# Attention and a long convolution on one core: the middle of every sixth VectorE exponential block computed on GpSimd

## The chip, the cores and the metric

The kernel runs on one core of a Trainium2 chip. The metric is the device time of one execution in microseconds (us). A core has a matrix engine (TensorE, PE in the profile), VectorE (DVE), ScalarE (ACT), GpSimd (POOL) and SyncE (SP), which only starts transfers here. Each engine works through its own list of instructions in order, and they wait for one another by semaphores. TensorE writes into PSUM, eight banks of 128 x 512 fp32; everything else lies in SBUF.

## The reference

Two independent halves are computed in bf16 and put side by side (S = 2048 rows, D = 512 columns each):

```python
# A: attention, 32 heads of 16 columns
qkv = x @ wqkv                      # q, k, v: [32, 2048, 16]
p = softmax(q @ k^T / 4)            # [32, 2048, 2048]
a = (p @ v) @ wo

# B: a gated convolution
kv = shift_conv(k, shift_k, 4 taps) * v
y = causal_conv(kv, ssm_k, 2048 taps per channel) + kv * ssm_D
b = q * y
out = concat([a, b], axis=-1)       # [2048, 1024]
```

## The kernel before

**Attention.** The score matrix is cut into 2048 blocks of 128 keys x 512 queries. A block takes a score matmul into a PSUM bank (L729), an exponential into SBUF, and a matmul with V (L795) that adds it to an accumulator bank. The softmax's denominators come out of the same matmul, from columns of ones beside V; a finished group of 64 blocks is transposed, divided and put away on VectorE (L820 to L835).

**The convolution** is 8192 small matmuls (L920) against rows of the kernel that SyncE loads, 512 loads of 512 KB (L903). They fill TensorE's time between score matmuls at a planned pace of one step (four matmuls) in `PACE` ns. VectorE moves results (L936, L962).

**Who does the exponential.** A step (`T`) has two or three blocks in neighbouring banks. ScalarE takes two or three of them in one instruction (L736). At some steps the third goes to VectorE instead, which computes 2^z in five passes (`exp_on_dve`): from PSUM to an integer that holds exponent and fraction (tile `EI`, L754), a linear pass over the low 16 bits into fp32 (tile `EM`, L757), twice a sum times itself in place (L759), and a last pass that adds the exponent and stores bf16 bits (tile `PTD`, L760):

```python
js = [job(... u = PA * f + PB ...)]            # L757
for c in (PC, PD): js.append(job(... u = (u + c) * u ...))   # L759
js.append(job(... PTD = ei * 2.0 ** -9 + u ...))             # L760
```

The first pass frees the PSUM bank, which the score matmuls two steps later need. `EI` and `PTD` have four buffers each, `EM` two.

**What sets the order.** All instructions of a core are laid out before the run by a planner in the same file. It keeps a clock for each engine with fixed costs (692 ns for a VectorE pass from PSUM, 427 for the linear one) and writes out each engine's list. VectorE's work consists of jobs with a due time; whenever the planned VectorE is free, `commit_one` takes the ready job that is due first. A block's last pass is due 7000 ns after its step's exponential. A step's third block is given to VectorE if the cost of all pending passes is below `DVE_OPEN` and enough blocks are left (`form`, L1138). The run follows the written order whatever the true times are.

**GpSimd** sets up masks and fills in the first 5 us. Later it only starts transfers: shifted rows of k, the q columns, `wo`, and the stores of output rows. In time it idles for most of the run.

Of the kernel before, what the change touches and what calls it, by code (L numbers as in the profile page):

```python
# [6 lines left out]
ALU = mybir.AluOpType  # L7
BF16 = mybir.dt.bfloat16
FP32 = mybir.dt.float32
INT32 = mybir.dt.int32  # L10
UINT16 = mybir.dt.uint16
# [30 lines left out]
PA, PB, PC, PD = -1.32672387e-05, -6.76483421, 6.76469236, -6.64090344  # L42
# [12 lines left out]
DVE_GAP = 2  # L55
DVE_OPEN = 3000.0
DVE_END = 48
PACE = 357.0
LAG_NS = 130.0
PE_SLACK = 850.0  # L60
PV_NS = 260.0
DMA_NS = 5600.0
N_TAIL = 9
# [75 lines left out]
def at_of(h):  # L139
    return 0.0 if h is None else Eng.at.get((id(h[0]), h[1]), 0.0)  # L140
# [13 lines left out]
def bass_concat_heads__mha_block__ssm_conv_h3__prompt_kernel(  # L154
# [21 lines left out]
    def sem(name):  # L176
        return enter(nc.semaphore(name))

    def sb(name, shape, dt=BF16):
        return enter(nc.sbuf_tensor(name, shape, dt))  # L180
# [12 lines left out]
    WKV = sb("WKV", [128, 2, 4, D])  # L193
# [8 lines left out]
    PTD = sb("PTD", [128, 4, QB])  # L202
    EI = sb("EI", [128, 4, QB], INT32)
    EM = sb("EM", [128, 2, QB], FP32)
    JNK = sb("JNK", [128, 2], FP32)
    WK = WKV[:, 0, :, :]
    WV = WKV[:, 1, :, :]
    WOP = WKV[:, 0, :, :]
    wr_flat = WR[:, :, :].rearrange("p r w -> p (r w)")
    KZS = wr_flat[:, 0:4 * LKZ].rearrange("p (c m) -> p c m", c=4)  # L210
# [12 lines left out]
    pe, act, dve, pool, sp = [Eng(sem(n), *k) for n, k in (("s_pe", (170.0,)), ("s_act", (100.0,)), ("s_dve", (-10.0, -85.0)),  # L223
                                                           ("s_pool", ()), ("s_sp", ()))]

    jobs = []
    WAIT = Job(None, (), 0.0, 0.0)

    def job(fn, deps, cost, due, then=None):
        j = Job(fn, deps, cost, due, then)  # L230
        jobs.append(j)
        return j

    def resolve(j):
        out = []
        for d in j.deps:
            d = d() if callable(d) else d
            if isinstance(d, Job):
                if d.h is None:
                    return None  # L240
                d = d.h
            out.append(d)
        return out

    def ready_of(j):
        deps = resolve(j)
        return None if deps is None else max([0.0] + [at_of(d) + 45.0 for d in deps if d is not None])

    def commit_one(until=None):
        found = [(ready_of(j), j) for j in jobs]  # L250
        found = [(r, j) for r, j in found if r is not None]
        if not found:
            return False
        t0 = max(dve.t, min(r for r, j in found))
        if until is not None and t0 >= until:
            return False
        j = min((j for r, j in found if r <= t0), key=lambda j: j.due)
        for r, u in sorted(((r, u) for r, u in found if u.due < j.due), key=lambda x: x[1].due):
            if r < t0 + j.cost and t0 + j.cost + u.cost + 80.0 > u.due:
                j = u  # L260
                break
        jobs.remove(j)
        j.h = dve.op(j.fn, resolve(j), cost=j.cost)
        if j.then:
            j.then(j.h)
        return True

    def advance(t):
        while commit_one(t):
            pass  # L270
# [36 lines left out]
    def dma(eng, dsem, outp, inp, deps=(), transpose=False):  # L307
        h = dsem.add()

        def fn(e):  # L310
            f = e.dma_start_transpose if transpose else e.dma_start
            f(outp, inp).then_inc(dsem.sem, 16)  # L312
        eng.op(fn, deps, inc=False)
        return h
# [18 lines left out]
    def load_x(eng, ds, t0, t1):  # L333
        return dma(eng, ds, KV[:, t0:t1, :], x2[t0 * 128:t1 * 128, :].rearrange("(t p) d -> p t d", p=128))

    def landing(h, us):
        Eng.at[(id(h[0]), h[1])] = 1000.0 * us
        return h
# [3 lines left out]
    h_wk = [landing(dma(act, d_w[1], WK[:, :, 0:128], wview[:, :, D:D + 128]), 5.4)]  # L342
    h_wv = landing(dma(act, d_w[2], WV, wview[:, :, 2 * D:3 * D]), 8.5)
    h_xn[1] = landing(load_x(sp, d_x[1], 4, 8), 8.5)
# [97 lines left out]
    def pe_unit(u, bank, dcs=(0, 1, 2, 3)):  # L442
        kind = u[0]
        deps = [bank_free[bank]]
        if kind == "q":
# [3 lines left out]
            def mm(e, dc):  # L449
                return e.matmul(PS[:, bank, :], lhsT=WQ[:, dc, o * 128:(o + 1) * 128], rhs=xT[:, dc, qb * 512:(qb + 1) * 512],  # L450
                                start=(dc == 0), stop=(dc == 3))
# [7 lines left out]
        else:  # L459
# [3 lines left out]
            def mm(e, dc):  # L463
                return e.matmul(PS[:, bank, :], lhsT=xT[:, dc, kt * 128:(kt + 1) * 128], rhs=WV[:, dc, :],  # L464
                                start=(dc == 0), stop=(dc == 3))
# [141 lines left out]
    def turn_first(cs, t0, dep):  # L607
        def fn(e):
            ins = None
            for c in cs:  # L610
                for t in range(t0, t0 + 2):
                    pbf = PS[:, first_bank[c], :].bitcast(BF16)
                    ins = e.transpose(pbf[:, 128 * t:128 * t + 128],
                                      KV[:, t, 128 * c:128 * c + 128], IDN[:, :])
            return ins
        return pe_op(fn, [dep, h_idn], full(128, 2 * len(cs)))
# [3 lines left out]
    for c in range(4):  # L620
        h = turn_first([c], 2, h_xn[0])
# [9 lines left out]
    def first_q(dc):  # L631
        return pe_op(lambda e: e.matmul(PS[:, 6, :], lhsT=WQ[:, dc, 0:128], rhs=xT[:, dc, 0:512],
                                        start=(dc == 0), stop=(dc == 3)), [h_x[0][dc], h_wq[0]], full(512, 1))

    def first_k(bank, c0, c1):
        def fn(e):
            ins = None
            for dc in range(4):
                ins = e.matmul(PS[:, bank, c0:c1], lhsT=WK[:, dc, 0:128], rhs=xT[:, dc, c0:c1],
                               start=(dc == 0), stop=(dc == 3))  # L640
            return ins
        return pe_op(fn, [*h_x[0], h_wk[0], bank_free[bank]], full(c1 - c0, 4))

    for dc in range(4):
        h = first_q(dc)
    evac_unit(("q", 0, 0), 6, h)
    h = first_k(7, 0, 128)
# [68 lines left out]
    h_blk = {}  # L716
# [28 lines left out]
    h_fix = {}  # L745
    h_ptd = {}
    h_pair = {}

    def exp_on_dve(b, bank, h, T):
        i = on_dve[b]  # L750
        u, ei = EM[:, i % 2, :], EI[:, i % 4, :]
        f = ei.bitcast(UINT16).rearrange("p (n h) -> p n h", h=2)[:, :, 0]
        end = at_of(h_exp[T])
        h_fix[i] = job(lambda e: e.tensor_scalar(ei, PS[:, bank, :], FIX_LO, FIX_ADD, ALU.max, ALU.add),  # L754
                       [h, h_pair.get(i - 4)], 692.0, end)
        due = end + 7000.0
        js = [job(lambda e: e.tensor_scalar(u, f, PA, PB, ALU.mult, ALU.add), [h_fix[i], h_pair.get(i - 2)], 427.0, due - 2400.0)]  # L757
        for c in (PC, PD):
            js.append(job(lambda e, c=c: e.scalar_tensor_tensor(u, u, c, u, ALU.add, ALU.mult), [js[-1]], 693.0, due + 700.0 * (len(js) - 3)))  # L759
        js.append(job(lambda e: e.scalar_tensor_tensor(PTD[:, i % 4, :].bitcast(UINT16), ei, 2.0 ** -9, u, ALU.mult, ALU.add),  # L760
                      [js[2], (lambda: h_ptd.get(i - 4, WAIT)) if i >= 4 else None], 693.0, due))
        h_pair[i] = h_blk[b] = js[-1]
        passes.extend(js)
        dve_wait.append(b)
        return h_fix[i]

    blk_on_dve = {}
    dve_wait = []
    passes = []
# [88 lines left out]
    def load_wop(h_last):  # L858
        h_wop[0] = dma(pool, d_wo, WOP, A_wo.rearrange("(o p) f -> p o f", p=128), [h_last])

    def op_mm(qb, t, j0, j1, bank):
# [3 lines left out]
        def fn(e):  # L865
            ins = None
            for j in range(j0, j1):
                ins = e.matmul(PS[:, bank, :], lhsT=OTN[:, (4 * qb + j) % R_O, t * 128:(t + 1) * 128], rhs=WOP[:, j, :],  # L868
                               start=(j == 0), stop=(j == 3))
# [160 lines left out]
    def emit_conv(T):  # L1030
# [10 lines left out]
        if not st["started"]:  # L1041
            fill(max(max(Mm.tile), pe.t), at_of(h_exp[T]) - PE_SLACK)
            st["now"] = at_of(h_exp[T])
            return
        limit = at_of(h_exp[T]) - PE_SLACK
        now = at_of(h_exp[T])
        ahead = [(st["wr"][i] + 1500.0 - now) / (NB * (i - st["qd"]) - st["lag"]) for i in range(st["qd"] + 1, len(st["wr"]))]
        st["lags"] = min(st["lags"] + (now - st["now"]) / max([PACE] + ahead), 2.0 * LAGS)
        st["now"] = now
# [44 lines left out]
    def emit_pv_dyn(T):  # L1094
        end = flow["NT"] is not None and T >= flow["NT"]
        limit = math.inf if end or T < T_DYN else at_of(h_exp[T]) - PE_SLACK
        while True:
# [72 lines left out]
    while flow["NT"] is None or T < flow["NT"] + 2:  # L1170
# [4 lines left out]
        if NT is None or T < NT:  # L1175
            u = form(T)
# [21 lines left out]
    while jobs:  # L1198
        assert commit_one()
# [8 lines left out]
    for t in range(4):  # L1208
        h = op_mm(qb, t, 3, 4, tail_banks[t])
# [55 lines left out]
```

## Time and profile before

| | |
|---|---|
| median of 3 runs | 877.3 us (876.84 to 877.31) |
| the profiled execution's own time | 873.7 us |
| its span, first to last instruction | 871.9 us |
| busy: ACT, DVE, PE, POOL | 846.1, 813.8, 711.0, 36.7 us |
| VectorE blocks (L754) | 226 of 2048 |
| ScalarE instructions (L736) | 368 of three blocks, 359 of two |
| mean granted TensorE clock | 0.974 |

The profile names a group of instructions by line, engine, operation and tiles (output<-input), with shape and count, then busy time and mean duration, then the idle time before them and what ended it. The chain of waits goes back from the last instruction to whatever released each step. The stretches (windows) give the busy time of each engine between two points of the span.

### The profile page before, as it was taken

What the parts mean: (1) busy time and instruction counts of PE and PEld (TensorE: products, weight loads), DVE (VectorE), ACT (ScalarE), POOL (GpSimd) and SP (SyncE); (2) the same over time, 40 slices, a digit from 0 to 9 for tenths busy, and PEclk for the clock granted to TensorE, in tenths of its full rate; (3) what the DMA queues carried; (4) which work ended last, traced back from release to release, by engine and by line L of the source; (5) the groups of instructions that cost most, each with busy time, mean ns of one, the idle gap of its engine ahead of it and who ended that gap; (6) DMA issues with size and microseconds to landing.
All of it is one profiled execution on the core that took longest, in us unless ns stands there. A gap on an engine that the chain in (4) does not pass through costs nothing.

```text
span 871.9 us, 28977 instructions
## 1 busy us (share of the span) xinstructions
PE 711.0 (82%) x12755; PEld 323.2 (37%) x12798; DVE 813.8 (93%) x1448; ACT 846.1 (97%) x733; POOL 36.7 (4%) x60
## 2 busy tenths in 40 slices
PE   8988978887888878777778787787778887877787
PEld 3322334443334433333334333333334343333331
DVE  3889999999989999999999999999999999999961
ACT  6999999999999999999999999999999999999996
POOL 3132000000000000000001000000000000000000
PEclk9999999999899999999999999999999999899996
DMA  9877699999999999999999999999999999999921
GB/s 315 294 251 269 201 356 350 379 395 354 373 324 354 353 371 360 380 368 380 354 381 379 374 387 371 349 382 361 371 373 361 372 378 394 320 367 362 382 75 43
DMA packets 88431, 295.63 MB, mean 339 GB/s; under 512 B 11125, under 2 KB 19314, under 8 KB 87922
## 3 DMA queue, kind: packets, MB, share of 16 engines
q1 hardware_dynamic: 82386, 280.00, 87.5%
q0 software_dynamic: 3776, 12.58, 4.3%
q8 instruction: 102, 1.67, 0.7%
q10 hardware_dynamic: 2144, 1.18, 0.5%
q14 instruction: 23, 0.19, 0.1%
HBM read 287.31 MB, written 6.42 MB: 337 GB/s over the span
## 4 chain that ended last, share of the span: by engine, by line
ACT 44%; DVE 41%; PE 12%; issue 2%; DMA 1%; ACTq 0%; DVEq 0%
ACT PT L736 44%; DVE EM L759 14%; DVE EI L754 8%; DVE PTD L760 8%; DVE EM L757 4%; PE PS L729 4%; PE PS L795 2%; PE PS L920 1%; DVE DT L820 1%; DVE YB L936 1%; DVE QT L485 1%; PE PS L464 1%; DMA WKV<-in_A_wqkv_dram 1%; PE PS L457 1%; PE PS L450 1%
## 5 line engine op out<-in xcount | busy, mean ns | idle before, releaser
L736 ACT ACTIVATE PT<-PS 128x1024 bf16<-128x1024 f32 (+1 forms) x727 | 842.6, 1386 | 14.3 <-PE PS L729 13.2
L729 PE MATMUL PS<-QT,KTo 32*128 32x512 bf16 x2048 | 290.2, 391 | 143.0 <-ACT PT L736 128.6
L759 DVE SCALAR_TENSOR_TENSOR EM<-EM 128x512 f32<-128x512 f32 x452 | 312.8, 714 | 0.6
L920 PE MATMUL PS<-WR,KV 128*16 128x128 bf16 (+15 forms) x8192 | 268.0, 226 | 0.3
L920 PEld LDWEIGHTS PS<-WR,KV 128*14 128x14 bf16 (+15 forms) x8192 | 193.5, 108 | 79.1 <-issue 42.5
L795 PE MATMUL PS<-PT,VAF 128*32 128x512 bf16 x1822 | 195.0, 398 | 1.9 <-ACT PT L736 0.8
L729 PEld LDWEIGHTS PS<-QT,KTo 32*128 32x128 bf16 x2048 | 72.0, 91 | 282.7 <-ACT PT L736 237.3
L760 DVE SCALAR_TENSOR_TENSOR PTD<-EI,EM 128x512 uint16<-128x512 int32 x226 | 161.0, 714 | 0.3
L754 DVE TENSOR_SCALAR EI<-PS 128x512 int32<-128x512 f32 x226 | 158.8, 703 | 1.4 <-PE PS L729 1.3
L757 DVE TENSOR_SCALAR EM<-EI 128x512 f32<-128x512 uint16 x226 | 97.8, 443 | 0.1
L795 PEld LDWEIGHTS PS<-PT,VAF 128*32 128x32 bf16 x1822 | 48.4, 93 | 112.1 <-issue 101.0
L795 PE MATMUL PS<-PTD,VAF 128*32 128x512 bf16 x226 | 79.3, 390 | 2.6 <-DVE PTD L760 2.0
L820 DVE STREAM_TRANSPOSE DT<-PS 128x512 f32<-128x512 f32 x31 | 23.2, 749 | 24.0 <-PE PS L795 23.6
L312 POOL DMA_DIRECT2D out_dram<-OUTA x12 | 6.6, 547 | 507.0 <-DVE OUTA L880 503.1
L795 PEld LDWEIGHTS PS<-PTD,VAF 128*32 128x32 bf16 x226 | 19.5, 95 | 21.6 <-DVE PTD L760 16.3
L936 DVE CAST YB<-PS 128x512 bf16<-128x512 f32 x32 | 21.9, 685 | 0.5 <-PE PS L920 0.4
L485 DVE TENSOR_TENSOR QT<-PS,MSK 128x1024 bf16<-128x1024 f32 x15 | 18.5, 1236 | 2.3 <-PE PS L450 1.8
L501 DVE CAST VAF<-PS 128x512 bf16<-128x512 f32 x16 | 11.0, 689 | 8.6 <-PE PS L464 8.4
L868 PE MATMUL PS<-WKV,OTN 128*128 128x512 bf16 x51 | 16.8, 425 | 2.6 <-issue 1.4
L464 PE MATMUL PS<-WKV,xT 128*128 128x512 bf16 x58 | 15.2, 381 | 1.7 <-issue 0.8
L457 PE MATMUL PS<-xT,WKV 128*128 128x512 bf16 x52 | 13.8, 381 | 1.1 <-issue 1.0
L450 PE MATMUL PS<-xT,WQ 128*128 128x512 bf16 x47 | 12.7, 381 | 2.2 <-issue 1.4
(69 smaller groups left out, 225.2 us busy)
## 6 DMA issues: line engine op xcount, KB each, us to landing
WR<-kz_scratch SPq DMA_DIRECT2D x512, 512.0 KB, 7.7
WR<-in_B_k_dram POOLq DMA_DIRECT2D x15, 256.0 KB, 7.4
kz_scratch<-WR SPq DMA_DIRECT2D x1, 2176.0 KB, 8.6
out_dram<-QN POOLq DMA_DIRECT2D x2, 1024.0 KB, 8.2
QT<-in_B_k_dram POOLq DMA_DIRECT2D x7, 256.0 KB, 8.7
KV<-in_A_x_dram SPq DMA_DIRECT2D x3, 512.0 KB, 8.4
out_dram<-OUTA POOLq DMA_DIRECT2D x12, 128.0 KB, 5.7
WR<-in_B_v_dram SPq DMA_DIRECT2D x5, 256.0 KB, 4.8
```

Of the source, the lines that this page charges most:

```text
L464: return e.matmul(PS[:, bank, :], lhsT=xT[:, dc, kt * 128:(kt + 1) * 128], rhs=WV[:, dc, :], start=(dc == 0), stop=(dc == 3))
L485: hh = dve_job(lambda e: e.tensor_tensor(QT[:, qb % 2, 2 * o:2 * o + 2, :], src, MSK[:, :, 0:1].broadcast_to([128, 2, QB]), ALU.mult), [h, ...
L729: ins = e.matmul(PS[:, bank, :], lhsT=KTo[32 * s:32 * s + 32, g // 2, kt * 128:(kt + 1) * 128], rhs=QT[32 * s:32 * s + 32, qb % 2, g, :], ...
L736: h_exp[T] = act.op(lambda e: e.activation(PT[:, T % R_PT, 0:n * QB], PS[:, banks[0]:banks[0] + n, :].rearrange("p b f -> p (b f)"), ACT.E ...
L754: h_fix[i] = job(lambda e: e.tensor_scalar(ei, PS[:, bank, :], FIX_LO, FIX_ADD, ALU.max, ALU.add), [h, h_pair.get(i - 4)], 692.0, end)
L757: js = [job(lambda e: e.tensor_scalar(u, f, PA, PB, ALU.mult, ALU.add), [h_fix[i], h_pair.get(i - 2)], 427.0, due - 2400.0)]
L759: js.append(job(lambda e, c=c: e.scalar_tensor_tensor(u, u, c, u, ALU.add, ALU.mult), [js[-1]], 693.0, due + 700.0 * (len(js) - 3)))
L760: js.append(job(lambda e: e.scalar_tensor_tensor(PTD[:, i % 4, :].bitcast(UINT16), ei, 2.0 ** -9, u, ALU.mult, ALU.add), [js[2], (lambda: ...
L795: ins = e.matmul(PS[32 * s:32 * s + 32, pvb(qb * NG + g), :], lhsT=VAF[:, kt, h * VW:h * VW + 32], rhs=rhs, start=first[b], stop=last[b], ...
L820: h_t = dve_job(lambda e: e.transpose(out=dt, in_=PS[:, pvb(n), :]), [h, h_mult.get(n - 2 if n == 2 else n - 1) if n != 1 else None], 717. ...
L920: ins = e.matmul(PS[32 * c:32 * c + NB - n, BGB, 128 * (kk % 4):128 * (kk % 4) + 128], lhsT=KV[:, n:NB, d], rhs=WR[:, d % R_W, 128 * (NB - ...
L936: bank_free[BGB] = dve_job(lambda e: e.tensor_copy(YB[:, half, :].rearrange("p (k i) -> p k i", k=4), src), [h, (lambda: h_yb.get(qd // 8 ...
```

## The change

Every sixth VectorE block (`G_EACH = 6`) is *shared*. VectorE still does its first and its last pass. The four operations between them are written as five instructions for GpSimd, in two fp32 tiles `GA` and `GB` that lie where the V weights stood (tile `WKV`, no longer read by then). As (u + PC) * u with u = PA * f + PB needs an operation of two kinds in one, GpSimd makes both factors by linear passes: `GA = PA f + PB`, `GB = PA f + PB + PC`, `GA = GA GB`, `GB = GA + PD`, `GA = GA GB`. The result is the same polynomial.

`feed_pool` puts the five on GpSimd's list as soon as the planner has committed the block's first pass on VectorE and the last pass of the shared block before it (which frees `GA`). It plans 600 ns for a linear pass and 1250 ns for a product. The last pass on VectorE waits for the fifth instruction. The `EM` buffers now rotate over the other blocks only. `PACE` goes from 357 to 352 ns.

```diff
-PACE = 357.0
+PACE = 352.0
+G_EACH = 6
...
+    GA, GB = [WKV[:, 1, 2 * i:2 * i + 2, :].rearrange("p a d -> p (a d)").bitcast(FP32) for i in range(2)]
...
+    hooks = []
...
     def commit_one(until=None):
...
         if j.then:
             j.then(j.h)
+        for f in hooks:
+            f()
         return True
...
+    h_own, h_shared, pool_wait = [], [], []
+    hooks.append(lambda: feed_pool())
+
+    def feed_pool():
+        while pool_wait and pool_wait[0][0].h is not None:
+            fx, f, q, n = pool_wait[0]
+            free = h_shared[n - 1].h if n else None
+            if n and free is None:
+                return
+            pool_wait.pop(0)
+            h = pool.op(lambda e: e.tensor_scalar(GA, f, PA, PB, ALU.mult, ALU.add), [fx.h, free], cost=600.0)
+            h = pool.op(lambda e: e.tensor_scalar(GB, f, PA, PB + PC, ALU.mult, ALU.add), [fx.h, free], cost=600.0)
+            h = pool.op(lambda e: e.tensor_tensor(GA, GA, GB, ALU.mult), [h], cost=1250.0)
+            h = pool.op(lambda e: e.tensor_scalar(GB, GA, 1.0, PD, ALU.mult, ALU.add), [h], cost=600.0)
+            q.h = pool.op(lambda e: e.tensor_tensor(GA, GA, GB, ALU.mult), [h], cost=1250.0)
...
     def exp_on_dve(b, bank, h, T):
         i = on_dve[b]
-        u, ei = EM[:, i % 2, :], EI[:, i % 4, :]
+        ei = EI[:, i % 4, :]
...
         due = end + 7000.0
-        js = [job(lambda e: e.tensor_scalar(u, f, PA, PB, ALU.mult, ALU.add), [h_fix[i], h_pair.get(i - 2)], 427.0, due - 2400.0)]
+        if i % G_EACH == G_EACH - 1:
+            q = Job(None, (), 0.0, 0.0)
+            pool_wait.append((h_fix[i], f, q, len(h_shared)))
+            h_shared.append(job(lambda e: e.scalar_tensor_tensor(PTD[:, i % 4, :].bitcast(UINT16), ei, 2.0 ** -9, GA, ALU.mult, ALU.add),
+                                [q, (lambda: h_ptd.get(i - 4, WAIT)) if i >= 4 else None], 693.0, due))
+            h_pair[i] = h_blk[b] = h_shared[-1]
+            passes.append(h_shared[-1])
+            dve_wait.append(b)
+            return h_fix[i]
+        m = len(h_own)
+        u = EM[:, m % 2, :]
+        js = [job(lambda e: e.tensor_scalar(u, f, PA, PB, ALU.mult, ALU.add), [h_fix[i], h_own[m - 2] if m > 1 else None], 427.0, due - 2400.0)]
```

Since the planner sees other costs, it writes another order. In the new one VectorE has 242 blocks, of which 40 are shared, and ScalarE has 352 instructions of three blocks and 375 of two.

VectorE around its eighth move of convolution results (`YB`), before:

```order
L757 TENSOR_SCALAR EM<-EI 128x512
L759 SCALAR_TENSOR_TENSOR EM<-EM 128x512 x2
L760 SCALAR_TENSOR_TENSOR PTD<-EI,EM 128x512
L759 SCALAR_TENSOR_TENSOR EM<-EM 128x512
L754 TENSOR_SCALAR EI<-PS 128x512
L760 SCALAR_TENSOR_TENSOR PTD<-EI,EM 128x512
L757 TENSOR_SCALAR EM<-EI 128x512
L936 CAST YB<-PS 128x512
L754 TENSOR_SCALAR EI<-PS 128x512
```

The same place now (`WKV` is the GpSimd result; lines have moved by some 22 to 34):

```order
L776 TENSOR_SCALAR EI<-PS 128x512
L792 SCALAR_TENSOR_TENSOR EM<-EM 128x512
L793 SCALAR_TENSOR_TENSOR PTD<-EI,EM 128x512
L776 TENSOR_SCALAR EI<-PS 128x512
L790 TENSOR_SCALAR EM<-EI 128x512
L792 SCALAR_TENSOR_TENSOR EM<-EM 128x512 x2
L970 CAST YB<-PS 128x512
L776 TENSOR_SCALAR EI<-PS 128x512
L782 SCALAR_TENSOR_TENSOR PTD<-EI,WKV 128x512
```

The first row is the first pass of the shared block, the last row its last pass; the eight instructions between them belong to other work. Over the 40 shared blocks 7 to 10 instructions stand between the two passes, together 73 first passes, 159 products (L792, L793), 43 linear passes (L790) and 59 others, 334 in all.

GpSimd's list, in the middle of the run, before:

```order
L312 DMA WKV<-in_A_wo_dram 128x4x512
L312 DMA out_dram<-OUTA 128x512 x7
L312 DMA out_dram<-QN 128x16x256
L312 DMA QN<-in_B_q_dram 128x16x256
L312 DMA out_dram<-OUTA 128x512 x5
```

The same place now, from the last chain before the second half of the q columns is loaded to the first one behind it:

```order
L769 TENSOR_TENSOR WKV<-WKV 128x512
L318 DMA out_dram<-OUTA 128x512 x2
L318 DMA out_dram<-QN 128x16x256
L318 DMA QN<-in_B_q_dram 128x16x256
L318 DMA out_dram<-OUTA 128x512 x2
L765 TENSOR_SCALAR WKV<-EI 128x512
L766 TENSOR_SCALAR WKV<-EI 128x512
L767 TENSOR_TENSOR WKV<-WKV 128x512
L768 TENSOR_SCALAR WKV<-WKV 128x512
L769 TENSOR_TENSOR WKV<-WKV 128x512
```

Transfers that GpSimd starts now stand in one list with 40 such chains of five.

More of the change, by code (lines that the diff above doesn't have):

```diff
@@ L762, in exp_on_dve @@
         h_pair[i] = h_blk[b] = js[-1]
+        h_own.append(js[-1])
         passes.extend(js)
```

## The prediction

> **What bounds the kernel now.** I first read the page's top and its chain of waits.
>
> ```profile
> span 871.9 us, 28977 instructions
> PE 711.0 (82%) x12755; PEld 323.2 (37%) x12798; DVE 813.8 (93%) x1448; ACT 846.1 (97%) x733; POOL 36.7 (4%) x60
> ACT 44%; DVE 41%; PE 12%; issue 2%; DMA 1%; ACTq 0%; DVEq 0%
> ```
>
> Two engines share the chain almost evenly; POOL does next to nothing. The shares are averages, so I then took the stretches from 110 us on, where exponentials, convolution and VectorE blocks all run (columns: us, then busy us and instructions of PE, PEld, DVE, ACT, POOL, then PEclk, DMA share, GB/s).
>
> ```profile
> 300.00:400.00 100.00, 79.24 (x1640) 38.20 (x1639) 99.83 (x178) 99.94 (x85) 0.00 (x0) 1.00 0.99 367
> 500.00:600.00 100.00, 79.09 (x1671) 37.39 (x1665) 99.61 (x178) 99.61 (x84) 0.00 (x0) 1.00 0.99 372
> sum 725.00, PE 585.94 PEld 279.96 DVE 712.63 ACT 717.05 POOL 9.64; mean PE 73.24 PEld 35.00 DVE 89.08 ACT 89.63 POOL 1.21
> ```
>
> From 110 to 835 us (the sum row) VectorE idles 725.00 - 712.63 = 12.4 us and ScalarE 8.0 us. Both are full. VectorE's first pass on a block frees the PSUM bank that a later score matmul needs, so a late VectorE makes TensorE and then ScalarE late. Unless work leaves VectorE on balance, the span cannot shrink; what VectorE gains beyond 12.4 us lengthens it one for one.
>
> The groups by shape give the prices (busy us, mean ns of one):
>
> ```profile
> L736 ACT ACTIVATE PT<-PS 128x1536 bf16<-128x1536 f32 x368 | 562.8, 1616 | 5.3 <-PE PS L729 4.7
> L736 ACT ACTIVATE PT<-PS 128x1024 bf16<-128x1024 f32 x359 | 399.3, 1150 | 9.0 <-PE PS L729 8.5
> L759 DVE SCALAR_TENSOR_TENSOR EM<-EM 128x512 f32<-128x512 f32 x452 | 312.8, 714 | 0.6
> L760 DVE SCALAR_TENSOR_TENSOR PTD<-EI,EM 128x512 uint16<-128x512 int32 x226 | 161.0, 714 | 0.3
> L754 DVE TENSOR_SCALAR EI<-PS 128x512 int32<-128x512 f32 x226 | 158.8, 703 | 1.4 <-PE PS L729 1.3
> L757 DVE TENSOR_SCALAR EM<-EI 128x512 f32<-128x512 uint16 x226 | 97.8, 443 | 0.1
> ```
>
> VectorE's instructions overlap at their ends, so a mean is more than one costs. The timeline (start us, us) shows the step:
>
> ```profile
> 300.87 0.67 DVE L760 SCALAR_TENSOR_TENSOR PTD<-EI,EM 128x512 uint16<-128x512 int32 x1
> 301.46 0.68 DVE L759 SCALAR_TENSOR_TENSOR EM<-EM 128x512 f32<-128x512 f32 x1
> 302.06 0.68 DVE L754 TENSOR_SCALAR EI<-PS 128x512 int32<-128x512 f32 x1
> 302.66 0.77 DVE L760 SCALAR_TENSOR_TENSOR PTD<-EI,EM 128x512 uint16<-128x512 int32 x1
> 303.35 0.47 DVE L757 TENSOR_SCALAR EM<-EI 128x512 f32<-128x512 uint16 x1
> 303.68 0.71 DVE L835 STREAM_TRANSPOSE OTN<-DTN 128x512 bf16<-128x512 bf16 x1
> ```
>
> Starts lie 0.60 us apart, and 0.33 after the linear pass (303.35 to 303.68). A VectorE block is one first pass, one linear pass and three products: 4 x 0.60 + 0.33 = 2.73 us.
>
> **The change, part by part.** *What VectorE loses.* A shared block keeps the first and last pass; 0.33 + 2 x 0.60 = 1.53 us go. There are 40 such blocks: -61 us.
>
> *What it gains.* The planner sees a lighter VectorE and hands it 242 blocks, not 226: 16 x 2.73 = +44 us. On balance VectorE has 17.5 us less.
>
> *ScalarE* loses these 16 blocks in as many instructions as before (352 of three blocks, 375 of two, 727 in all). One block more in an instruction costs 1616 - 1150 = 466 ns, so 16 cost 7.5 us; ends overlap here too, so I take 7.
>
> *GpSimd's chain.* Five operations in series replace the three passes: two linear passes, product, linear pass, product. POOL's rows near them are small ones:
>
> ```profile
> L402 POOL TENSOR_SCALAR_AFFINE_SELECT IDN<-IDN 128x128 bf16<-128x128 bf16 x1 | 0.3, 292 | 0.0
> L396 POOL TENSOR_SCALAR_AFFINE_SELECT MSK<-MSK 128x8 f32<-128x8 f32 x2 | 0.4, 188 | 0.1
> L400 POOL TENSOR_TENSOR MSK<-MSK 128x2 f32<-128x2 f32 x3 | 0.6, 195 | 0.2
> 1.66 0.74 POOL L400 TENSOR_TENSOR MSK<-MSK 128x2 f32<-128x2 f32 x3
> ```
>
> One input: (292 - 188) / 120 = 0.87 ns an element, so 512 elements take 292 + 384 x 0.87 = 0.63 us. Two inputs: the floor is 0.19 us, and an element costs one such step at least (0.64 us in all), three at most for two reads and a write (1.52 us); I take two, 1.08 us, for two reads. The hand-over from one to the next is (740 - 195) / 2 - 195 = 78 ns. The chain: 3 x 0.63 + 2 x 1.08 + 4 x 0.08 = 4.4 us, between 3.5 and 5.3.
>
> The Trainium skill (GPSIMD Engine Reference, Performance versus the Vector engine) measured 4497 ns for a two-input add of 2048 fp32 elements; a quarter is 1.12 us, an estimate that would make the chain 4.5 us. No run here shows it yet.
>
> *The cover.* VectorE works in order, and the last pass of a shared block waits for POOL. Between a shared block's first and last pass the new order puts 7 to 10 VectorE instructions, over the 40 blocks 8.35 on average: 1.8 first passes, 4.0 products, 1.1 linear passes and 1.5 others (transposes, casts, small ones; about 0.8 us together). That is 1.1 + 2.4 + 0.35 + 0.8 = 4.6 us after the first pass's own step of 0.60, or 4.5 us from its end. So the chain just fits on average, and where only 7 instructions stand there it is some 0.7 us late. Without any interference I expect 0.2 us of waiting a block, 8 us in all (0 at 3.5 us of chain; 0.75 us a block, 30 us, at 5.3). Behind the waiting pass stand the next first passes, and so PSUM banks, score matmuls and ScalarE.
>
> *The interference.* What does POOL cost VectorE when both read SBUF? No row has it: POOL's only reads lie before 2.7 us, with VectorE nearly idle. The nearest is a POOL fill, which only writes, beside two-input VectorE products:
>
> ```profile
> 78.42 2.65 POOL L369 MEMSET QT<- 3x3072 bf16 x1 [13.18 <-DVE KV L558]
> 80.11 1.28 DVE L538 TENSOR_TENSOR WR<-WR 128x1024 bf16<-128x1024 bf16 x2
> L538 DVE TENSOR_TENSOR WR<-WR 128x1024 bf16<-128x1024 bf16 x20 | 13.2, 680 | 0.0
> ```
>
> The fill stretched nothing (2 in 1.28 us, against a mean of 680 ns with overlapped ends). So the lower bound is 0. The upper: the engines take turns for each whole instruction. VectorE's rows say why that is possible. The linear pass from SBUF does 512 elements in 0.33 us, the first pass from PSUM in 0.60; so with one SBUF input VectorE draws two elements in a step. The products draw one element from each of two inputs in a step. Both thus use two SBUF reads a step, and no VectorE row uses more. POOL's reads come on top. If they need one of those two paths, the 4.0 products and 1.1 linear passes of a window (2.4 + 0.35 us, and the small two-input ones, 2.8 in all) cannot run beside POOL's 4.4 us. Then the last pass starts 2.8 + 4.4 = 7.2 us after the first, not 4.5: 2.7 us of delay a block. If an operation's fixed 0.19 us needs no path, five of them give 0.95 back: 1.75 us. It does not matter who goes first: either VectorE's products wait for POOL, or POOL starts late and the last pass waits for it. I take the middle, 2.2 us, because I see no third read in any row: 40 x 2.2 = +88 us.
>
> The Trainium skill has such a rule (SBUF — State Buffer, Who interferes with whom): a VectorE instruction with two SBUF inputs, or in a two-port mode, contends with a GpSimd instruction that reads SBUF, and the one that comes second is held for the whole instruction, while GpSimd writes do not disturb two-input ones. The fill above agrees with the last part (2 in 1.28 us); by the whole rule the delay would be the full 2.7 us, 107 us in all, and the time 962. The reading part is shown by no run here.
>
> *POOL's queue.* The stores of output rows and the load of queries now stand between chains. That load waits for the store ahead of it:
>
> ```profile
> 477.42 1.17 POOL L312 DMA_DIRECT2D out_dram<-QN  x1 [4.03 <-DVE QN L962]
> 488.12 1.16 POOL L312 DMA_DIRECT2D QN<-in_B_q_dram  x1 [9.53 <-DMA out_dram<-QN]
> ```
>
> Behind it a chain can begin 12 us late, but the next first pass of a shared block comes 19 VectorE instructions (10 us) after that store's product. I charge nothing; without that distance it would be 10 us, once.
>
> *The sum.* VectorE: -17.5 + 88 = +70.5 us. Its old idle time can take up to 12.4 of that; I let it take 5, since most of that idle time lies where groups end. ScalarE's 7 us are then no gain, since it waits for VectorE. The profiled execution took 873.7 us (span 871.9); the median of the runs shown is 877.3, 3.6 above. 877.3 + 65.5 = **943 us**.
>
> **The rivals.** *A: no interference.* VectorE has 17.5 - 8 = 9.5 us less and stays behind ScalarE, which has 7 us less: 870 us (867 to 875). For it: the fill beside the products. Against it: it is a write. Here the convolution would have to run faster too, since its pace is set to 352 ns a step instead of 357:
>
> ```profile
> WR<-kz_scratch SPq DMA_DIRECT2D x512, 512.0 KB, 7.7
> ```
>
> Four such loads for 16 steps are 2.1 MB in 5.63 us, 372 GB/s; the stretches above moved 367 and 372 at a DMA share of 0.99. If that is the ceiling, some 3 us of the 7 are lost.
>
> *B: the chain is merely slow, or only one kind of pass takes turns.* With 5.3 us of chain and no interference, 30 us of waiting: -17.5 + 30 = +12.5, 890 us. If only the 1.1 linear passes of a window take turns with POOL (0.35 us of them plus 0.2 of waiting a block): 40 x 0.55 - 17.5 = +4.5, 882 us. It decides from 0.44 us of delay a block on (17.5 / 40). For it: two-input prices on POOL are extrapolated from 2 elements. I say 885 us.
>
> *C: the change does not do what it says,* because POOL is never ready and VectorE waits out each chain: 4.4 us against 1.53 saved would be the forecast again by another name, since the cover of 4.5 us is there in the order; no price of its own.
>
> **How the numbers follow.** Taking turns 0.48 (917 to 967: 40 x 1.75 or 2.7, less 17.5, less 12.4 or 0); B 0.19; A 0.33. A measurement of this kernel can tell about 0.2%, 1.8 us, from no change. A gives faster 0.30 and same 0.03; B, in its milder forms, same 0.04 and slower 0.15; the forecast is all slower: faster 0.30, same 0.07, slower 0.63. The range reaches from inside A to the forecast's upper end, 868 to 967; the forecast's own is 917 to 967.
>
> **What would show it.** Right: VectorE's products and linear passes stretch, or start late, while POOL is busy, and first passes from PSUM do not; the last passes at the new line wait for POOL; POOL's operations are longer than 0.63 and 1.08 us or start late; ScalarE idles for score matmuls. Wrong: products at 714 ns beside POOL's operations, no wait at the shared last pass, and ScalarE still full from 300 to 600 us. A chain above 5 us with unstretched products is B.

## The result and the profile after

The changed kernel takes 963.1 us (median of 6 runs, 957.1 to 968.3) against 877.1 for the kernel before (6 runs on the same chip, 873.6 to 878.3). The ratio is 1.100, with a 95% interval of 1.095 to 1.104: 10% slower. The forecast was 943 us, and its own range of 917 to 967 holds the time. The profiled execution took 957.1 us.

The page's top, after:

```profile
span 955.4 us, 29154 instructions
PE 773.4 (81%) x12798; PEld 338.2 (35%) x12798; DVE 880.1 (92%) x1408; ACT 850.8 (89%) x733; POOL 270.3 (28%) x260
DVE 59%; PE 20%; ACT 12%; POOL 4%; DMA 2%; issue 2%; ACTq 0%; DVEq 0%
```

VectorE was to do less (1408 instructions instead of 1448), yet its busy time rose from 813.8 to 880.1 us. In the chain of waits it now has 59% instead of 41, and ScalarE 12% instead of 44. One of the stretches shown before says it by stage (us, then busy us of PE, PEld, DVE, ACT and POOL, then PEclk, DMA share, GB/s):

```profile
300.00:400.00 100.00, 78.70 (x1423) 36.44 (x1416) 96.36 (x148) 85.82 (x74) 27.04 (x24) 0.88 0.90 323
```

In 100 us VectorE gets 148 instructions done instead of 178, and ScalarE 74 instead of 85. VectorE is nearly as busy as it was: its instructions have become longer on average. The groups by shape show which:

```profile
L742 ACT ACTIVATE PT<-PS 128x1536 bf16<-128x1536 f32 x352 | 523.1, 1518 | 59.4 <-PE PS L735 58.6
L742 ACT ACTIVATE PT<-PS 128x1024 bf16<-128x1024 f32 x375 | 389.9, 1074 | 33.1 <-PE PS L735 32.0
L792 DVE SCALAR_TENSOR_TENSOR EM<-EM 128x512 f32<-128x512 f32 x404 | 314.6, 789 | 1.6
L776 DVE TENSOR_SCALAR EI<-PS 128x512 int32<-128x512 f32 x242 | 167.4, 692 | 9.0 <-PE PS L735 8.7
L793 DVE SCALAR_TENSOR_TENSOR PTD<-EI,EM 128x512 uint16<-128x512 int32 x202 | 154.0, 763 | 0.5
L790 DVE TENSOR_SCALAR EM<-EI 128x512 f32<-128x512 uint16 x202 | 112.0, 556 | 0.5
...
L863 DVE TENSOR_TENSOR DTN<-DT,DR 128x256 bf16<-128x256 f32 x31 | 17.6, 566 | 0.1
...
L869 DVE STREAM_TRANSPOSE OTN<-DTN 128x512 bf16<-128x512 bf16 x15 | 10.7, 712 | 0.0
```

The first pass from PSUM (L776) is 692 ns against 703 before. The passes with two inputs in SBUF are longer (the products 789 and 763 against 714, the small product L863 566 against 425), and so is the linear pass, 556 against 443. The transpose from SBUF to SBUF (L869) is not: 712 against 736 (L835 before). ScalarE idles 90.6 us for score matmuls, against 13.2. The mean of the products hides two kinds (duration in ns: least, median, most):

```profile
L792 DVE SCALAR_TENSOR_TENSOR EM<-EM x404: 623/692/1925, 98.6 to 926.3; 128x512 f32<-128x512 f32 x135
```

The median is an ordinary duration, so a minority is much longer. Worked out from the trace, the 96 products of L792 that overlap an operation of a GpSimd chain take 1067 ns on average and the other 308 take 703; for the linear pass it is 1041 and 425, for the first pass 697 and 690. The timeline shows how. VectorE and POOL around the first shared block (start us, us):

```profile
111.10 0.72 DVE L776 TENSOR_SCALAR EI<-PS 128x512 int32<-128x512 f32 x1
...
112.47 0.99 DVE L792 SCALAR_TENSOR_TENSOR EM<-EM 128x512 f32<-128x512 f32 x1
113.39 0.72 DVE L776 TENSOR_SCALAR EI<-PS 128x512 int32<-128x512 f32 x1
113.99 0.70 DVE L793 SCALAR_TENSOR_TENSOR PTD<-EI,EM 128x512 uint16<-128x512 int32 x1
114.62 1.50 DVE L863 TENSOR_TENSOR DTN<-DT,DR 128x256 bf16<-128x256 f32 x1
116.03 0.87 DVE L790 TENSOR_SCALAR EM<-EI 128x512 f32<-128x512 uint16 x1
116.94 1.63 DVE L792 SCALAR_TENSOR_TENSOR EM<-EM 128x512 f32<-128x512 f32 x1
118.49 0.68 DVE L776 TENSOR_SCALAR EI<-PS 128x512 int32<-128x512 f32 x1
119.09 0.67 DVE L782 SCALAR_TENSOR_TENSOR PTD<-EI,WKV 128x512 uint16<-128x512 int32 x1
```

```profile
111.92 1.01 POOL L765 TENSOR_SCALAR WKV<-EI 128x512 f32<-128x512 uint16 x1 [12.86 <-DVE EI L776]
113.02 0.93 POOL L766 TENSOR_SCALAR WKV<-EI 128x512 f32<-128x512 uint16 x1
114.03 1.80 POOL L767 TENSOR_TENSOR WKV<-WKV 128x512 f32<-128x512 f32 x1
115.91 0.71 POOL L768 TENSOR_SCALAR WKV<-WKV 128x512 f32<-128x512 f32 x1
116.70 1.31 POOL L769 TENSOR_TENSOR WKV<-WKV 128x512 f32<-128x512 f32 x1
```

Read the two side by side. POOL's product runs until 115.83, and VectorE's small product L863, which takes 0.43 us in a kernel without the chains (first experiment), takes 1.50 and ends at 116.12. POOL's second product ends at 118.01; VectorE's product L792 began at 116.94, as that product was under way, and ends only at 118.57, 0.56 us later. The first passes at 113.39 and 118.49, which read PSUM, are not longer. POOL is held too: its first product overlaps L793, which ends at 114.69, and takes 1.80 us, 0.53 more than the least that this product takes.

### The profile page after: what moved, and what is told of

The parts are those of the page before. It is cut to its first block, busy times and chain, and to the rows that moved or that the text cites. A ratio compares the mean times of both kernels' runs of the same rounds, so it can differ in the third digit from the quotient of the medians.

```text
span 955.4 us, 29154 instructions
## 1 busy us (share of the span) xinstructions
PE 773.4 (81%) x12798; PEld 338.2 (35%) x12798; DVE 880.1 (92%) x1408; ACT 850.8 (89%) x733; POOL 270.3 (28%) x260
## 4 chain that ended last, share of the span: by engine, by line
DVE 59%; PE 20%; ACT 12%; POOL 4%; DMA 2%; issue 2%; ACTq 0%; DVEq 0%
DVE EM L792 20%; ACT PT L742 12%; DVE EI L776 11%; DVE PTD L793 10%; DVE EM L790 7%; PE PS L735 7%; PE PS L954 5%; PE PS L829 4%; DVE PTD L782 2%; DVE DT L854 2%; DVE QT L491 2%; DVE YB L970 1%; DVE DTN L863 1%; PE PS L456 1%; DMA out_dram<-QN 1%
## 5 line engine op out<-in xcount | busy, mean ns | idle before, releaser
L742 ACT ACTIVATE PT<-PS 128x1024 bf16<-128x1024 f32 (+1 forms) x727 | 847.2, 1289 | 92.5 <-PE PS L735 90.6
L735 PE MATMUL PS<-QT,KTo 32*128 32x512 bf16 x2048 | 309.5, 418 | 128.0 <-ACT PT L742 84.0
L792 DVE SCALAR_TENSOR_TENSOR EM<-EM 128x512 f32<-128x512 f32 x404 | 314.6, 789 | 1.6
L954 PE MATMUL PS<-WR,KV 128*6 128x128 bf16 (+15 forms) x8192 | 292.2, 237 | 6.7 <-DVE YB L970 5.2
L954 PEld LDWEIGHTS PS<-WR,KV 128*8 128x8 bf16 (+15 forms) x8192 | 202.2, 110 | 96.2 <-issue 64.9
L765 POOL TENSOR_SCALAR WKV<-EI 128x512 f32<-128x512 uint16 x40 | 42.0, 1050 | 522.7 <-DVE EI L776 522.6
L776 DVE TENSOR_SCALAR EI<-PS 128x512 int32<-128x512 f32 x242 | 167.4, 692 | 9.0 <-PE PS L735 8.7
L793 DVE SCALAR_TENSOR_TENSOR PTD<-EI,EM 128x512 uint16<-128x512 int32 x202 | 154.0, 763 | 0.5
L829 PE MATMUL PS<-PTD,VAF 128*32 128x512 bf16 x242 | 92.5, 429 | 31.9 <-DVE PTD L793 20.1
L790 DVE TENSOR_SCALAR EM<-EI 128x512 f32<-128x512 uint16 x202 | 112.0, 556 | 0.5
L767 POOL TENSOR_TENSOR WKV<-WKV 128x512 f32<-128x512 f32 x40 | 62.6, 1564 | 3.3
L769 POOL TENSOR_TENSOR WKV<-WKV 128x512 f32<-128x512 f32 x40 | 60.6, 1514 | 3.3
L766 POOL TENSOR_SCALAR WKV<-EI 128x512 f32<-128x512 uint16 x40 | 33.9, 848 | 3.2
L768 POOL TENSOR_SCALAR WKV<-WKV 128x512 f32<-128x512 f32 x40 | 33.5, 837 | 3.5
L782 DVE SCALAR_TENSOR_TENSOR PTD<-EI,WKV 128x512 uint16<-128x512 int32 x40 | 27.6, 689 | 5.1 <-POOL WKV L769 5.1
```

The costliest lines, as they stand in the source:

```text
L735: ins = e.matmul(PS[:, bank, :], lhsT=KTo[32 * s:32 * s + 32, g // 2, kt * 128:(kt + 1) * 128], rhs=QT[32 * s:32 * s + 32, qb % 2, g, :], ...
L742: h_exp[T] = act.op(lambda e: e.activation(PT[:, T % R_PT, 0:n * QB], PS[:, banks[0]:banks[0] + n, :].rearrange("p b f -> p (b f)"), ACT.E ...
L765: h = pool.op(lambda e: e.tensor_scalar(GA, f, PA, PB, ALU.mult, ALU.add), [fx.h, free], cost=600.0)
L767: h = pool.op(lambda e: e.tensor_tensor(GA, GA, GB, ALU.mult), [h], cost=1250.0)
L769: q.h = pool.op(lambda e: e.tensor_tensor(GA, GA, GB, ALU.mult), [h], cost=1250.0)
L782: h_shared.append(job(lambda e: e.scalar_tensor_tensor(PTD[:, i % 4, :].bitcast(UINT16), ei, 2.0 ** -9, GA, ALU.mult, ALU.add), [q, (lambd ...
```

## The experiments

The theory: GpSimd and VectorE take turns in reading SBUF, so each chain holds VectorE's two-input products and linear passes. Its rivals for a loss of 86 us: the new order or the pace of 352 ns is bad in itself; VectorE waits at the last pass for a slow chain; GpSimd's work costs VectorE whatever it does to SBUF (any write, or a fixed price for an instruction and its semaphore).

**The order without the chains.** The planner keeps its times for GpSimd, so each instruction of the other engines stands where the change puts it, but the five operations are not issued. A constant from one fill stands for GpSimd's result.

```diff
-            h = pool.op(lambda e: e.tensor_scalar(GA, f, PA, PB, ALU.mult, ALU.add), [fx.h, free], cost=600.0)
...
-            q.h = pool.op(lambda e: e.tensor_tensor(GA, GA, GB, ALU.mult), [h], cost=1250.0)
+            h = gp.op(None, [fx.h, free], cost=600.0)
...
+            q.h = gp.op(None, [h], cost=1250.0)
+            if n == 0:
+                h_fill.append(pool.op(lambda e: e.memset(GA, -7.0), [fx.h]))
```

> The changed kernel in the same order on VectorE, TensorE and ScalarE, but GpSimd's 40 chains are left out: one fill puts a constant where their result stands, and the last pass of a shared block waits for nothing on GpSimd (so the middle of the shared blocks is not computed). Turns (the two engines cannot read SBUF side by side): 866 to 874 us, VectorE 17.5 us lighter than before and ScalarE 7. Late chain (the loss is the wait of the last pass for a chain that is too long): the same 866 to 874. Order (the new order, the faster convolution pace or the lower granted clock that goes with them costs the time): 940 or more.

Measured: 864.2 us, ratio 0.987 (0.981 to 0.993), 1.8 us below the lower end that was expected. Its groups, the spread of the products, and one stretch:

```profile
L800 DVE SCALAR_TENSOR_TENSOR EM<-EM 128x512 f32<-128x512 f32 x404 | 285.1, 717 | 1.6
L801 DVE SCALAR_TENSOR_TENSOR PTD<-EI,EM 128x512 uint16<-128x512 int32 x202 | 142.8, 707 | 0.5
L798 DVE TENSOR_SCALAR EM<-EI 128x512 f32<-128x512 uint16 x202 | 88.1, 438 | 0.5
L871 DVE TENSOR_TENSOR DTN<-DT,DR 128x256 bf16<-128x256 f32 x31 | 13.3, 429 | 0.1
```

```profile
L800 DVE SCALAR_TENSOR_TENSOR EM<-EM x404: 622/694/950, 98.5 to 834.4; 128x512 f32<-128x512 f32 x135
```

```profile
300.00:400.00 100.00, 81.86 (x1654) 39.69 (x1650) 98.38 (x174) 99.60 (x86) 0.00 (x0) 0.98 1.00 373
```

Without the chains every pass has its old duration and ScalarE is full again. The order and the pace are innocent: with VectorE's three middle passes gone from 40 blocks (three, not four as the section on the change has it), they would have made the kernel 1.3% faster. The chains alone cost (1.0996 - 0.9874) x 877 = 98 us, 2.46 us for each of 40.

**Writes instead of reads.** The chain becomes five fills of about the same lengths, so GpSimd is as long in use and the last pass still waits for the fifth. GpSimd reads nothing, and its result is a constant.

```diff
...
+            h = pool.op(lambda e: e.memset(FILL[:, 0:612], -7.0), [fx.h, free], cost=600.0)
+            h = pool.op(lambda e: e.memset(FILL[:, 0:612], -7.0), [fx.h, free, h], cost=555.0)
+            h = pool.op(lambda e: e.memset(FILL[:, 0:1286], -7.0), [h], cost=1250.0)
+            h = pool.op(lambda e: e.memset(FILL[:, 0:612], -7.0), [h], cost=600.0)
+            q.h = pool.op(lambda e: e.memset(FILL[:, 0:1286], -7.0), [h], cost=1250.0)
```

> The changed kernel in the same order, but the five GpSimd instructions of a chain are fills of the same unhindered length (0.62 and 1.27 us), which write and read nothing; the last pass still waits for the fifth (the middle of the shared blocks is not computed). Turns, if only reads collide: 868 to 880 us, products at their 0.60 us step beside a fill, a wait of some 0.2 to 0.4 us a block. Turns, if the fast linear pass collides with writes too: up to 900. Late chain: the chain is as long as GpSimd's own work, so the wait stays: 940 or more. Order: 940 or more.

Measured: 881.8 us, ratio 1.009 (1.005 to 1.012). Its groups, and the linear pass alone (duration in ns: least, median, most):

```profile
L793 DVE SCALAR_TENSOR_TENSOR EM<-EM 128x512 f32<-128x512 f32 x404 | 282.6, 710 | 1.6
L794 DVE SCALAR_TENSOR_TENSOR PTD<-EI,EM 128x512 uint16<-128x512 int32 x202 | 141.4, 700 | 0.5
L791 DVE TENSOR_SCALAR EM<-EI 128x512 f32<-128x512 uint16 x202 | 100.4, 499 | 0.5
```

```profile
L791 DVE TENSOR_SCALAR EM<-EI x202: 384/424/1678, 100.7 to 850.1; 128x512 f32<-128x512 uint16 x101
```

Fills of about the chain's lengths leave the products alone (710 and 700 ns). So of the 98 us, 80 need GpSimd's reads: (1.0996 - 1.0085) x 877. The other 18 come with the writes: the linear pass has a median of 424 ns but single ones of up to 1678, and its 202 passes gained 61 ns each, 12 us. The fast pass is held by writes too, the two-input products are not.

**Chains that nobody waits for.** The kernel before in its own order, with 37 chains of GpSimd that compute on other data (the tile `xT`, no longer used). No result is used, so VectorE never waits for GpSimd.

```diff
...
         h_fix[i] = job(lambda e: e.tensor_scalar(ei, PS[:, bank, :], FIX_LO, FIX_ADD, ALU.max, ALU.add),
-                       [h, h_pair.get(i - 4)], 692.0, end)
+                       [h, h_pair.get(i - 4)], 692.0, end, idle_chain if i % 6 == 5 else None)
```

> The kernel before in its own order, and GpSimd computes a chain of the same five instructions at the first pass of every sixth VectorE block, 37 in all, on data of its own; nobody waits for them and the result is not used. Turns: each chain delays VectorE by about 2.5 us as in the changed kernel, 37 x 2.5 = 92, less up to 12 of idle time: 950 to 970 us. Late chain: nobody waits, 875 to 880. Order: unchanged, 875 to 880.

Measured: 965.8 us, ratio 1.101 (1.092 to 1.109). That is 0.1009 x 877 / 37 = 2.4 us a chain (2.2 to 2.6), as much as in the changed kernel. Its groups:

```profile
L770 DVE SCALAR_TENSOR_TENSOR EM<-EM 128x512 f32<-128x512 f32 x452 | 345.5, 785 | 0.6
...
L765 DVE TENSOR_SCALAR EI<-PS 128x512 int32<-128x512 f32 x226 | 157.3, 696 | 7.2 <-PE PS L731 6.7
L768 DVE TENSOR_SCALAR EM<-EI 128x512 f32<-128x512 uint16 x226 | 125.5, 564 | 0.1
```

The same passes are longer by nearly the same amounts (785 and 564 ns), and the first pass is not (696). The wait of the last pass for the chain is not what costs: here there is none, and the loss a chain is the same within its interval.

**Half as many chains.** Every twelfth block is shared: 19 chains, and the planner gives VectorE 234 blocks.

```diff
-G_EACH = 6
+G_EACH = 12
```

> The changed kernel with every twelfth VectorE block shared, pace 352 as in the change: 19 chains, 234 VectorE blocks. Turns: 19 x (2.5 - 1.53) + 8 x 2.73 = +40 us on VectorE, less up to 12 of idle time: 905 to 920. Late chain: per chain too, 905 to 920. Order: does not go with the number of chains, 940 or more.

Measured: 919.6 us, ratio 1.052 (1.044 to 1.060). That is 45 us over the kernel before with 19 chains, against 86 with 40: the loss grows with the number of chains. Per chain it is 2.4 and 2.15 us, but each sum also holds what its own order gains without chains, which was run for the 40 alone.

**Chains of short reads.** The same five operations with the same semaphores, but from the second chain on on 32 of the 512 columns, so that most of the shared blocks' polynomial is left out.

```diff
+            w = 32 if n else QB
-            h = pool.op(lambda e: e.tensor_scalar(GA, f, PA, PB, ALU.mult, ALU.add), [fx.h, free], cost=600.0)
+            h = pool.op(lambda e, w=w, f=f: e.tensor_scalar(GA[:, 0:w], f[:, 0:w], PA, PB, ALU.mult, ALU.add), [fx.h, free], cost=600.0)
...
```

> The changed kernel in the same order; from the second chain on, GpSimd's five instructions work on the first 32 of 512 columns only (the rest of a shared block's middle is not computed). They are as many, they read SBUF and wait for one another as before, but each is near its floor of 0.2 us. Turns, priced by the time that GpSimd reads: some 0.2 us a chain left, 866 to 878 us. A fixed price for each collision (200 GpSimd instructions cost the 100 us, 0.5 us each): 940 or more.

Measured: 869.5 us, ratio 0.994 (0.990 to 0.997), which is 0.0063 x 877 = 5.5 us over the kernel without chains, 0.14 us a chain. The two intervals overlap (0.990 to 0.997, 0.981 to 0.993), so even this is not clear of nothing. Two of its groups, and the start of one chain:

```profile
L766 POOL TENSOR_SCALAR WKV<-EI 128x32 f32<-128x32 uint16 x39 | 25.0, 642 | 548.1 <-DVE EI L777 548.1
...
L793 DVE SCALAR_TENSOR_TENSOR EM<-EM 128x512 f32<-128x512 f32 x404 | 284.7, 716 | 1.6
```

```profile
302.68 0.67 DVE L794 SCALAR_TENSOR_TENSOR PTD<-EI,EM 128x512 uint16<-128x512 int32 x1
302.84 0.59 POOL L766 TENSOR_SCALAR WKV<-EI 128x32 f32<-128x32 uint16 x1 [15.96 <-DVE EI L777]
```

VectorE's products are at 716 ns again. A price per instruction is out: the loss goes with the time that GpSimd reads. GpSimd's own first pass takes 642 ns on average for 32 columns, against 0.22 us at least. In the lines shown it ends 0.08 us after VectorE's product, as if it had waited for it.

**Linear passes alone.** The two products of the chain become linear passes of the same size, so that GpSimd reads one input in all five operations, and the shared blocks get another polynomial.

```diff
-            h = pool.op(lambda e: e.tensor_tensor(GA, GA, GB, ALU.mult), [h], cost=1250.0)
+            h = pool.op(lambda e: e.tensor_scalar(GA, GB, 1.0, PD, ALU.mult, ALU.add), [h], cost=1250.0)
...
-            q.h = pool.op(lambda e: e.tensor_tensor(GA, GA, GB, ALU.mult), [h], cost=1250.0)
+            q.h = pool.op(lambda e: e.tensor_scalar(GA, GB, 1.0, PD, ALU.mult, ALU.add), [h], cost=1250.0)
```

> The changed kernel in the same order, but the two products of a GpSimd chain are linear passes (0.62 us instead of 1.27), so a chain is 5 x 0.62 + 0.3 = 3.4 us unhindered instead of 4.7 and reads one input each time (the middle of the shared blocks is not computed rightly). Turns, priced by time: from the first pass's end to the last pass 7.0 - 1.3 = 5.7 us, 1.2 more than without GpSimd; 40 x 1.2 - 17.5 = +30: 895 to 915. A fixed price for each collision: 940 or more. Only two-input GpSimd instructions collide: 866 to 878.

Measured: 916.8 us, ratio 1.048 (1.043 to 1.054), 1.8 us above the upper end that was expected. Its groups:

```profile
L792 DVE SCALAR_TENSOR_TENSOR EM<-EM 128x512 f32<-128x512 f32 x404 | 297.9, 749 | 1.6
...
L790 DVE TENSOR_SCALAR EM<-EI 128x512 f32<-128x512 uint16 x202 | 101.0, 502 | 0.5
```

Against the kernel without chains that is (1.0484 - 0.9874) x 877 / 40 = 1.3 us a chain. One-input passes of GpSimd hold VectorE's products as well (749 ns against 717). Two products in place of two such passes, 2.5 us of GpSimd's work instead of 1.2, make the other 1.1 us.

**Delay without GpSimd.** The kernel before, with four more products on VectorE, in series and on unused data, behind the first pass of every sixth block (37 of them); the planner does not know of them. This puts a known delay where the chains put theirs.

```diff
...
+        for _ in range(4):
+            h = dve.op(lambda e: e.scalar_tensor_tensor(GB, GA, PC, GA, ALU.add, ALU.mult), [h])
...
```

> The kernel before in its own order, without GpSimd work; behind the first pass of every sixth VectorE block stand four more products of VectorE on data of its own, 4 x 0.60 = 2.4 us, 37 times, in place of the collisions. If a VectorE that is late by that much explains all of the loss, the granted clock too: 37 x 2.4 = 89 us on 877, 950 to 966, with a mean granted clock of 0.90 to 0.92 as in the changed kernel. If GpSimd's work itself lowers the clock: 940 to 955 and a clock of 0.95 or more.

Measured: 1000.0 us, ratio 1.142 (1.137 to 1.148), far above both cases that were expected, with a granted clock of 0.876, below both. One reason is the size of the delay:

```profile
112.57 0.68 DVE L761 TENSOR_SCALAR EI<-PS 128x512 int32<-128x512 f32 x1
113.28 2.90 DVE L753 SCALAR_TENSOR_TENSOR WKV<-WKV 128x512 f32<-128x512 f32 x4
116.10 0.68 DVE L766 SCALAR_TENSOR_TENSOR EM<-EM 128x512 f32<-128x512 f32 x1
```

Without the four, the next product would start 0.60 us after 112.57; it starts at 116.10, 2.93 us later, not 2.4: these products, each of which waits for the one before it, don't overlap at their ends (2.90 us for four). That makes 37 x 2.93 = 108 us. The kernel lost 122, 1.13 times as much: here the delay is passed on in full, and something comes on top.

**A version that beats both.** If VectorE's passes are what is scarce, the gain lies in fewer of them, not in another engine. In the kernel before, every second VectorE block gets a polynomial of degree two instead of three: a linear pass, one product and the last pass. The pace is 352 ns, and the planner gives VectorE 250 blocks. This changes what is computed: 2^z is off by up to 0.17% in those blocks.

```diff
-PACE = 357.0
+PACE = 352.0
+QA, QBB, QC = 1.002448577e-04, -6.63719769, 6.60393536
+SHORT = 2
...
-        for c in (PC, PD):
+        pa, pb, cs = (QA, QBB, (QC,)) if i % SHORT == 0 else (PA, PB, (PC, PD))
+        for n, c in enumerate(cs):
...
```

> The kernel before without any GpSimd work: every second VectorE block takes a polynomial of degree two, one product less (0.60 us), with a relative error of up to 0.17% in these blocks' exponentials; pace 352. The planner then gives VectorE 250 blocks instead of 226 and ScalarE 1798. If VectorE and ScalarE together bound the kernel: ScalarE loses 24 blocks x 0.45 = 11 us, VectorE 125 x 0.60 = 75 less 24 x 2.73 = 66, so 862 to 868. If the convolution's loads bound it at this pace: 870 or more.

> The kernel of the short polynomial on every second VectorE block once more, with more rounds, since its interval of 0.979 to 0.992 was wide: a ratio of 0.983 to 0.990 if VectorE and ScalarE together bound the kernel.

Measured: 861.0 us, ratio 0.985 (0.979 to 0.992), 1 us below the range that was expected, and in five further rounds 862.2 us, 0.984 (0.981 to 0.988). One stretch:

```profile
300.00:400.00 100.00, 79.96 (x1655) 38.31 (x1657) 99.82 (x181) 100.00 (x86) 0.00 (x0) 1.00 1.01 373
```

VectorE and ScalarE are both full, with 181 and 86 instructions instead of 178 and 85. It is 1.6% faster than the kernel before, in exchange for accuracy. The polynomial and the pace were changed together; neither was run alone.

## Why the prediction was right

**The mechanism was the predicted one, and its parts are shown.** Turn-taking at reads: the fills cost 18 of the 98 us, the idle chains 2.4 us each where the changed kernel's cost 2.46, the short reads next to nothing. (The fill at 78.42 us, from which the prediction took its lower bound, shows that GpSimd's fills don't all lie in the first 5 us; the section on the kernel before says that they do.) Rival A (no interference) was priced a little high for its case, 870 us (867 to 875), since the kernel without chains takes 864 (866 by its ratio), but the case did not come. Its doubt about a ceiling of the loads at 372 GB/s falls: that kernel is done earlier at the new pace, and single slices of its page, 21.6 us each, move up to 408 GB/s. Rival B (a slow chain, or only the linear passes take turns) falls: the products are held, and chains that nobody waits for cost as much.

The Trainium skill (SBUF — State Buffer, Who interferes with whom) states a rule that the runs bear out: a VectorE instruction with two SBUF inputs contends with a GpSimd instruction that reads SBUF and not with one that only writes it, and one in a two-port mode contends with GpSimd. The trace agrees for the products, 789 ns beside the chains and 710 beside fills (717 without either); the linear pass behaves as the second part says, 556 and 499 against 438.

The prediction gave 962 us for turns in full (877.3 - 17.5 + 107 - 5), and 963 were measured. That closeness is luck: turns in full meant a hold of 107 us, and the hold was 78, while another term was off the other way, as the next account shows. What a measurement can tell from no change was put too fine as well, at 0.2%: the interval of the ratio is 0.4% to either side.

**Where the 83.5 us of span went.** VectorE's busy time and the rest of the span, from the pages' tops; the kernel without chains is this:

```profile
span 862.5 us, 28955 instructions
PE 716.7 (83%) x12798; PEld 324.8 (38%) x12798; DVE 801.8 (93%) x1408; ACT 838.0 (97%) x733; POOL 37.9 (4%) x61
```

| term | predicted | measured |
|---|---|---|
| VectorE's passes removed and added | -17.5 | 801.8 - 813.8 = -12.0 |
| GpSimd's hold on VectorE | +88 | 880.1 - 801.8 = +78.3 |
| VectorE's idle time | -5 | 75.3 - 58.1 = +17.2 |
| sum | +65.5 | +83.5 |

*The hold* of 2.2 us a block was nearly right: from the end of a shared block's first pass to the start of its last one it is 7.0 us on average over the 40 blocks, and 5.1 in the kernel without chains, worked out from the traces: 1.9 us, within the bounds of 1.75 and 2.7. The full turns would have put the last pass 7.2 us after the first. The cover of 4.5 us was really 5.1, and the chain was longer than 4.4. GpSimd's durations (least, median, most, ns):

```profile
L765 POOL TENSOR_SCALAR WKV<-EI x40: 617/1010/1708, 111.9 to 917.5; 128x512 f32<-128x512 uint16 x40
L766 POOL TENSOR_SCALAR WKV<-EI x40: 620/934/1082, 113.0 to 918.6; 128x512 f32<-128x512 uint16 x40
L767 POOL TENSOR_TENSOR WKV<-WKV x40: 1266/1492/3421, 114.0 to 919.6; 128x512 f32<-128x512 f32 x40
L768 POOL TENSOR_SCALAR WKV<-WKV x40: 621/849/1310, 115.9 to 921.1; 128x512 f32<-128x512 f32 x40
L769 POOL TENSOR_TENSOR WKV<-WKV x40: 1265/1577/1927, 116.7 to 921.9; 128x512 f32<-128x512 f32 x40
```

The least is 0.62 us for a linear pass (0.63 predicted) and 1.27 for a product (1.08 predicted). Unhindered, the chain is then 3 x 0.62 + 2 x 1.27 + 4 x 0.08 = 4.7 us, still inside the cover; as it ran, it took 6.1 us on average (5.5 to 7.4), worked out from the trace. The estimate of 1.12 us for a product, a quarter of 4497 ns by the Trainium skill (GPSIMD Engine Reference, Performance versus the Vector engine), was too low too. VectorE's other passes were held meanwhile, so one sign that was named hardly showed, the wait of the last pass (us, times, the longest):

```profile
DVE PTD L782 <- POOL WKV L769: 5.1, 5, 1.6
```

The last pass waited for GpSimd 5 times in 40, for 5.1 us in all. The prediction said that it doesn't matter who goes first; here it was VectorE's other passes that were held, and by the time the last pass came the chain was done in 35 of 40 blocks.

*The term that was wrong* is the idle time: "I let it take 5". VectorE's old idle time took up nothing; it grew, from 58.1 us to 75.3, and is 862.5 - 801.8 = 60.7 in the kernel without chains. Of the 14.6 us above that kernel, 5.1 are the waits for GpSimd at the last pass and 3.5 are longer waits of the first pass for score matmuls (L776 idled 9.0 us, 5.5 without the chains, 1.4 before); the rest is spread over small waits. One reading is that the delay comes in lumps of some 2 us, TensorE and ScalarE fall behind, and later VectorE waits for score matmuls that they owe it. The four extra products fit this and need no GpSimd: VectorE's busy time rose there from 813.8 to 916.6 us, the span by 122, so that idle time rose by 19.4. The idle chains do not: VectorE's busy time rose there by 84.3, to 898.1 us in a span of 958.4, and its idle time only by 2.2. So the old idle time took up nothing of the delay in any of these runs; how much it grows, and why, stays open. "What VectorE gains lengthens the span one for one" was nearly exact for the idle chains (86.5 us of span for 84.3) and too mild for the extra products (122 for 108). The idle term, 22 us off, is larger than the 18 us by which the sum was short; the hold (10 less than predicted) and the removed passes (5.5 us less gain) make up the rest.

Nothing was charged for POOL's queue, and next to nothing shows there: 39 of the 40 chains start 0.1 us after their first pass and one 1.3 us after it.

## What to carry to other kernels

Before work goes to GpSimd, ask what the engine it is taken from does meanwhile: if that is VectorE, busy with two-input or fast passes on SBUF, some 4.7 us of GpSimd work cost it about 2 us and the kernel 2.46, more than the 1.53 us that were saved. Work on GpSimd was nearly free where it read little (0.14 us a chain of 32 columns), and VectorE's passes from PSUM were not held (692 ns). Where VectorE has no room, shorten its work (a product less in half its blocks, with a faster pace, gave 1.6%), and price a delay of VectorE at its full length at least.

## What the runs showed of the hardware

**The granted clock is lower in the longer runs, with GpSimd at work or not.** By the profiles it is 0.983 in a span of 862.5 us (the kernel without chains), 0.903 in 955.4 (the changed one) and 0.876 in 994.1, the one with four more products on VectorE. The kernel before has 871.9 us at 0.974; the other experiments on GpSimd have 866.1 at 0.980, 883.3 at 0.955, 910.4 at 0.947, 914.3 at 0.938 and 958.4 at 0.906. The lowest belongs to a kernel without any GpSimd work in its middle, so GpSimd is not needed for it. That the clock falls because TensorE waits more is a reading, not shown: executions of one kernel differ the same way (the kernel before in 867.1 us at 0.987, and in 877.5 at 0.958). How much of the extra 13% in the run with four more products is the slower clock and how much the waiting itself was not separated, and stays open.

**A short instruction can be the one that waits.** With 32 columns an operation of GpSimd takes 0.22 us at least, but its first pass 642 ns on average, and VectorE lost nearly nothing (its products took 716 ns): the short reader paid with its own time.
